# Where the last layer splits its operands: conversions once per step, token operands spread over two steps

## The chip, the cores and the metric

The kernel runs on one core of a Trainium2 chip. The metric is the device time of one execution in microseconds (us), the median of three runs.

## What is computed

Attention with a threshold, a mixture of eight experts, and a gated layer, one after the other. Only the last one, `_moe2_ref`, is touched by the change. Its input is the experts' output, 2304 tokens of width 512.

```python
def reference(**kwargs):
    ...
    attn_out = _attn_ref(**attn_kwargs)
    x = np.ascontiguousarray(attn_out.transpose(0, 2, 1, 3)).reshape(B * S, H * D)
    x = _moe_ref(x=x, **moe_kwargs)
    return _moe2_ref(x=x, **moe2_kwargs)

def _moe2_ref(x, w_gate, w_val, w_out):      # (2304, 512), (512, 1536) twice, (1536, 512)
    g = x @ w_gate
    silu = g * (1.0 / (1.0 + np.exp(-g)))
    val = x @ w_val
    return (silu * val @ w_out).astype(np.float32)
```

## The kernel before, around the change

**Tiling.** `moe2` (line 1533) works on the transposed tokens in groups of 384, taken as three pairs p = 0, 1, 2, and on the 1536 hidden units in 12 slices k of 128. Every float32 operand is split into a high and a low part (names ending in h and l: ScalarE casts the high part, VectorE subtracts to get the low one), so a product of two operands is three matmuls per chunk of 256 rows, and `product` (line 1623) issues six.

**Steps.** The list `steps` is one long sequence. The first 14 steps are `plain` ones (slices 0 to 6 of pair 0, one group each, four products). Then come 29 steps `seven`: slices 7 to 11 of pair 0, then 12 slices each of pairs 1 and 2. A `seven` step does two groups with seven products instead of eight; for that it needs sums of tokens (`ysum`: t1 to t4, from the loaded quarters r0 to r3) and sums of weights (`sums`, on GpSimd, into one buffer sf). The order of its products on TensorE is fixed: tokens y0, y2, yt2, yt1, yt3, y3, yt4 (tiles `p`, only two PSUM banks in turn). Between them stand 18 matmuls of the third product (tiles `o`, function `l2`) for the slice of the step before. A PSUM bank is free for the next product when the VectorE or ScalarE instruction that reads it is done: y0 by the copy at line 1665, y2 by `s<-p,p`, yt2 by `p<-p,p`, yt1 by the copy at line 1680, yt3 by `u<-p,p`, y3 by `s<-p,s`, yt4 by `u<-u,p`.

**Lists.** A `seven` step calls `at(pos)` at the places 0, 1, "u", 2, "t", 3, 4, 5, in this order, and at each of them all that the table `do[i, pos]` holds is issued, so the table sets the order of work on ScalarE, VectorE, GpSimd and the DMA queue (SP). Each engine takes its instructions strictly in that order. The table holds: weights of slice k+3 fetched from DRAM (wf), sums of slice k+2 (sf), the split of slice k+1 (`opers_hi` on ScalarE: ch; `opers_lo` on VectorE: cl; 512 wide for products y0 and y2, 256 wide for yt4, 1024 wide from sf for the other four), and, in the last steps of a pair, loads, sums and splits of the next pair's tokens (`yload`, `ysum`, `yhi`, `ylo`; 768 wide).

**Conversions.** The weights arrive as 64-bit floats. `Weights2.begin` issues, on ScalarE, the high part of a word tile that is ready (oh or ch from wb, line 1476) and the scaling of a raw tile (line 1452); `end` issues, on VectorE, the low part (line 1477) and the three word operations on the tile just scaled (lines 1457 to 1459). In the `seven` steps before the change, places 0 and 3 both do `end`, `begin(1)`, `fill`:

```python
            if i >= n0 and pos in (0, 3):
                w2s.end()
                w2s.begin(1)
                w2s.fill()
```

**Stores.** At slice 11, `store` (line 1592) copies six output tiles out of PSUM and GpSimd issues an indirect DMA for each; two of them use the tag eys, four the tag os.

Of the kernel before, what the change touches and what calls it, by code (L numbers as in the profile page):

```python
# [6 lines left out]
F32 = mybir.dt.float32  # L7
# [607 lines left out]
def apart(tc, group, ins):  # L615

    tc.declare_no_dep(ins.ins, group=group, reason="rows apart")
    tc.add_to_no_dep_group(group, ins.ins)
# [904 lines left out]
GT = 384  # L1523
# [13 lines left out]
def moe2(ctx, tc, w2s, yd, idl, out, y0, py0, pys):  # L1537
    nc = tc.nc
    p = lambda n, b, **kw: ctx.enter_context(tc.tile_pool(name=n, bufs=b, reuse_waits="tile", **kw))
    py, pr, pu, po, pi = p("n_y", 1), p("n_yr", 1), p("n_u", 2), p("n_o", 1), p("n_i", 1)  # L1540
# [5 lines left out]
    idf = pi.tile([128, 18], F32, name="idf")  # L1546
    nc.sync.dma_start(idf[:], idl[0:NTOK, 0:1].rearrange("(t p) o -> p (t o)", p=128))
    idi = pi.tile([128, 18], I32, name="idi")
    nc.vector.tensor_copy(idi[:], idf[:])
    V, S, G = nc.vector, nc.scalar, nc.gpsimd  # L1550
    tt = lambda e, o, a, b, op: e.tensor_tensor(o, a, b, op=op)  # L1551

# [1 line left out]
    Y, R = dict(y0), {}  # L1554

    def yload(p, b):
        R[b, p] = t = pr.tile([128, 2, GT], F32, tag=f"r{b}", name=f"r{b}")
        r, n = 256 * (b // 2), GT * (2 * p + b % 2)
        nc.sync.dma_start(t[:], yd[r:r + 256, n:n + GT].rearrange("(c p) n -> p c n", p=128))

    def ysum(p, n):
        a, b = {"t1": (1, 0), "t2": (3, "t1"), "t3": (3, 1), "t4": ("t2", 2)}[n]

        t = R[1, p] if n == "t3" else R[2, p] if n == "t4" else pr.tile([128, 2, GT], F32, tag="r" + n, name="r" + n)
        tt(V, t[:], R[a, p][:], R[b, p][:], ALU.subtract)
        R[n, p] = t

# [10 lines left out]
    def l2(g, k, order):  # L1578

        uh, ul = H.pop((g, k))  # L1580
        oh, ol = W["o", k]
        if k == 0:
            O[g] = [pso.tile([128, 512], F32, tag="o", name="o") for _ in range(3)]
        for t in range(3):
            sl = slice(128 * t, 128 * t + 128)
            for i, (u, w) in enumerate(((uh, oh), (uh, ol), (ul, oh))):
                nc.tensor.matmul(O[g][t][:], u[:, sl], w, start=k == 0 and i == 0, stop=k == NF - 1 and i == 2)  # L1587
                yield
            if k == NF - 1:
                store(g, t)  # L1590

    def store(g, t):
        i = 3 * g + t
        o = po.tile([128, 512], F32, tag="os", name="os", bufs=4) if i % 3 else pys.tile([128, 512], F32, tag="eys", name="os", bufs=2)
        (S.copy if i % 2 else V.tensor_copy)(o[:], O[g][t][:])
        ins = nc.gpsimd.indirect_dma_start(
            out=out[:, :], out_offset=bass.IndirectOffsetOnAxis(ap=idi[:, i:i + 1], axis=0),
            in_=o[:], in_offset=None, bounds_check=NTOK - 1, oob_is_err=False)
        apart(tc, "out", ins)
# [34 lines left out]
    def plain(g, k, i, at):  # L1634
        res = []
        for nm in (0, 2):
            ps = bank()
            for c in (0, 2):
                product(ps, [t[:, nm + c // 2] for t in w2s.C[k]], Y[c + g % 2, g // 2], c == 0, c == 2)
            res.append(ps)  # L1640
            at(nm // 2)
        s = pu.tile([128, GT], F32, tag=f"s{g % 2}", name="s", bufs=1)
        S.activation(s[:], res[0][:, 0:GT], AF.Silu)
        w2s.begin(2 if i % 2 or i > 11 else 1)
        hidden(g, k, s, res[1][:, 0:GT])()
        w2s.end()
        w2s.fill()
        rest()
        at(2)
        pend.append(l2(g, k, 0))  # L1650
        w2s.done += g
# [60 lines left out]
    steps = []  # L1712
    for k in range(PLAIN + LAG):
        steps += [(g, k - LAG * g) for g in range(2) if 0 <= k - LAG * g < PLAIN]
    n0 = len(steps)
    steps += [(p, k) for p in range(3) for k in range(0 if p else PLAIN, NF)]
    do = defaultdict(list)
    add = lambda i, pos, *what: do[i, pos].append(what)
    for b in (1, 3, 0, 2):
        yload(0, b)  # L1720
    for i, b in ((1, 1), (2, 3)):
        add(i, 2, yhi, 0, b)
        add(i + (b == 1), 0 if b == 1 else 2, ylo, 0, b)
    for i, b in ((n0 - 6, "t1"), (n0 - 5, "t2"), (n0 - 4, "t3")):
        add(i, 0, ysum, 0, b)
        add(i + 1, 0, yhi, 0, b)
        add(i + 1, 2, ylo, 0, b)
    add(n0 - 2, 0, ysum, 0, "t4")
    add(n0, 0, yhi, 0, "t4")
    add(n0, 1, ylo, 0, "t4")  # L1730
# [7 lines left out]
    for i in range(n0, len(steps)):  # L1738
        p, k = steps[i]
        if i + 3 < len(steps):  # L1740
            add(i, 0, w2s.fetch, steps[i + 3][1])
        if i + 2 < len(steps):
            add(i, 2, w2s.sums, steps[i + 2][1])
        if i + 1 < len(steps):
            k1 = steps[i + 1][1]
            for n in (0, 2, 1):
                add(i, 0, w2s.opers_hi, k1, n)
            for n, pos in ((0, 0), (1, 1), (2, "u")):
                add(i, pos, w2s.opers_lo, k1, n)
        if p < 2:  # L1750
            if k == 8:
                for b in (0, 1, 2, 3):
                    add(i, 0, yload, p + 1, b)
            if k > 8:
                add(i, "t", ysum, p + 1, f"t{k - 8}")
            if k == 11:
                for pos, b in ((1, 0), (2, 2), ("t", "t2"), (3, "t1"), (4, "t3")):
                    add(i, pos, yhi, p + 1, b)
                    add(i, pos, ylo, p + 1, b)
                for pos, b in ((0, 3), ("t", "t4")):  # L1760
                    add(i + 1, pos, yhi, p + 1, b)
                    add(i + 1, pos, ylo, p + 1, b)
                add(i + 1, 1, ysum, p + 1, "t4")
    for i, (g, k) in enumerate(steps):
        def at(pos):
            if i >= n0 and pos in (0, 3):
                w2s.end()
                w2s.begin(1)
                w2s.fill()
            for what, *x in do.pop((i, pos), ()):  # L1770
                what(*x)
        (plain if i < n0 else seven)(g, k, i, at)
# [38 lines left out]
def body(tc, q, k, v, tau, emb, mtau, w1, w2, wg, wv, wo, out):  # L1811
    nc = tc.nc
    with ExitStack() as top:
# [100 lines left out]
        with ExitStack() as ctx:  # L1914
            ctx.enter_context(tc.manual_schedule())
            moe2(ctx, tc, w2s, yd, idl, out, y0, py0, c)
# [26 lines left out]
```

## Time and profile before

| | us |
|---|---|
| three runs, median (lowest to highest) | 1081.05 (1079.9 to 1081.9) |
| the profiled execution: its time | 1085.99 |
| its span | 1084.0 |
| TensorE busy in the span | 1028.1 (95%) |
| VectorE, ScalarE, GpSimd busy | 786.0, 576.9, 318.9 |
[...]

The last layer's first plain step begins 604 us into the span. The chain that ended last goes through TensorE for 50% of the span and through VectorE for 9%. A busy TensorE is not TensorE at its peak; what a stage may give is read from its own windows and waits.

### The profile page before, as it was taken

The page shows a single profiled execution, that of the slowest core. Times are in us where ns is not written, and L with a number is a line of the kernel's source. Part 1 is how long each engine was busy: PE and PEld are TensorE (multiplying, and loading weights), DVE is VectorE, ACT ScalarE, POOL GpSimd, SP SyncE. Part 2 cuts the span into 40 slices and gives each one's busy share as a digit, 9 for nine tenths or more (in the row PEclk, how much of TensorE's full clock was granted, in tenths as well). Part 3 has the DMA queues.
Part 4 walks back from the last instruction along what each step waited for, and adds up shares of the span by engine and source line. Part 5 has one row for each costly group of instructions (what it writes and reads, how often), then busy time and mean ns, then how long its engine had stood idle before and what let it go on. Part 6 is the DMA issues. An engine that isn't in the chain of part 4 may idle for free.

```text
span 1084.0 us, 18612 instructions
## 1 busy us (share of the span) xinstructions
PE 1028.1 (95%) x6338; PEld 892.5 (82%) x6338; DVE 786.0 (73%) x1624; ACT 576.9 (53%) x1152; POOL 318.9 (29%) x451
## 2 busy tenths in 40 slices
PE   7999999999998899999999989868899999899996
PEld 6777777776767899999999989757789999799995
DVE  6888888888886445666677458867887778877773
ACT  5777777777772434555565434343454344434432
POOL 6444534446786000000000000211352323442222
PEclk9999999999999999999999989978999999899999
DMA  8679988756832657887897545750122132121101
GB/s 183 157 193 230 204 232 204 191 128 173 229 88 79 206 142 218 223 275 232 235 237 193 159 132 175 243 185 19 40 98 59 40 98 59 49 88 40 40 1 58
DMA packets 141008, 158.12 MB, mean 146 GB/s; under 512 B 53912, under 2 KB 96920, under 8 KB 140912
## 3 DMA queue, kind: packets, MB, share of 16 engines
q1 hardware_dynamic: 138032, 147.47, 50.4%
q0 software_dynamic: 2880, 9.46, 2.3%
q8 instruction: 50, 0.82, 0.3%
q14 instruction: 46, 0.38, 0.1%
HBM read 97.28 MB, written 34.06 MB: 121 GB/s over the span
## 4 chain that ended last, share of the span: by engine, by line
PE 50%; DVE 9%; ACT 3%; issue 2%; DMA 2%; SPq 0%; POOL 0%; POOLq 0%; DVEq 0%; ACTq 0%
PE p L1628 20%; PE o L1587 11%; PE y L1271 9%; PE ph L1253 9%; DVE s L1551 1%; DVE wb L1458 1%; PE pxt L1221 1%; DVE cl L1518 1%; DVE wb L1457 1%; DMA ws<-wb 1%; DVE wb L1459 1%; DMA wf<-ws 0%; ACT uh L1620 0%; DVE u L1551 0%; DVE w1l L1209 0%
## 5 line engine op out<-in xcount | busy, mean ns | idle before, releaser
L1494 POOL TENSOR_TENSOR sf<-wf 128x256 f32<-128x256 f32 x29 | 27.1, 936 | 565.4 <-DVE wb L1459 331.5
L196 DVE TENSOR_REDUCE nmx<-PS 128x1 f32<-128x576 f32 x144 | 108.8, 755 | 53.7 <-PE PS L165 41.3
L230 DVE SCALAR_TENSOR_TENSOR E<-PS,thr,E 128x576 f32<-128x576 f32 x128 | 103.4, 808 | 0.1
L290 ACT COPY h<-PS 128x256 f32<-128x256 f32 (+2 forms) x176 | 67.0, 381 | 66.5 <-PE PS L247 62.7
L220 ACT ACTIVATE E<-PS,nmx 128x576 f32<-128x576 f32 x128 | 96.1, 750 | 4.4 <-DVE nmx L196 2.7
L1258 DVE SCALAR_TENSOR_TENSOR hl<-ph,hh 128x256 fp32r<-128x256 f32 (+5 forms) x64 | 30.9, 483 | 79.8 <-ACT hh L1257 79.8
L165 PE MATMUL PS<-KH,qs 128*128 128x288 f32 x256 | 87.0, 354 | 1.7 <-ACT h L290 1.5
L1587 PE MATMUL o<-ol,uh 128*128 128x512 f32 x216 | 87.3, 404 | 0.0
L1587 PE MATMUL o<-oh,ul 128*128 128x512 f32 x216 | 86.8, 402 | 0.1
L1587 PE MATMUL o<-oh,uh 128*128 128x512 f32 x216 | 86.7, 401 | 0.0
L314 PE MATMUL y<-h,nv 128*64 128x320 f32 (+2 forms) x528 | 86.4, 419 | 0.0
L247 PE MATMUL PS<-ident,E 128*128 128x128 f32 x576 | 85.2, 275 | 1.2 <-DVE E L230 1.0
L1271 PE MATMUL y<-hh,w2h 128*128 128x256 f32 (+5 forms) x256 | 79.4, 310 | 0.0
L165 PEld LDWEIGHTS PS<-KH,qs 128*128 128x128 f32 x256 | 48.5, 190 | 36.9 <-ACT h L290 14.0
L1271 PE MATMUL y<-hl,w2h 128*128 128x256 f32 (+5 forms) x256 | 78.0, 305 | 0.0
L1271 PE MATMUL y<-hh,w2l 128*128 128x256 f32 (+5 forms) x256 | 77.9, 304 | 0.0
L247 PEld LDWEIGHTS PS<-ident,E 128*128 128x128 f32 x576 | 66.6, 140 | 10.4 <-issue 6.9
L165 PE MATMUL PS<-KL,qs 128*128 128x288 f32 x256 | 73.2, 298 | 0.0
L1696 ACT ACTIVATE s<-s 128x384 f32<-128x384 f32 x29 | 15.2, 524 | 106.3 <-DVE s L1551 106.3
L1620 ACT CAST uh<-s 128x384 fp32r<-128x384 f32 x72 | 36.9, 513 | 57.6 <-DVE s L1551 57.2
L1257 ACT ACTIVATE hh<-ph 128x256 fp32r<-128x256 f32 (+5 forms) x64 | 27.7, 433 | 71.1 <-PE ph L1253 67.1
L1551 DVE TENSOR_TENSOR s<-p,s 128x384 f32<-128x384 f32 x72 | 40.3, 559 | 27.2 <-ACT s L1696 16.0
(387 smaller groups left out, 3022.7 us busy)
## 6 DMA issues: line engine op xcount, KB each, us to landing
w1r<-in_moe_w_dram SPq DMA_DIRECT2D x32, 512.0 KB
w2r<-in_moe_w_dram SPq DMA_DIRECT2D x32, 512.0 KB
wf<-ws SPq DMA_DIRECT2D x58, 256.0 KB
xs<-zero SPq DMA_DIRECT2D x8, 1542.0 KB
KH<-tkh SPq DMA_DIRECT2D x60, 144.0 KB
KL<-tkl SPq DMA_DIRECT2D x60, 144.0 KB
rg<-in_moe_w_gate_dram SPq DMA_DIRECT2D x12, 512.0 KB
rv<-in_moe_w_val_dram SPq DMA_DIRECT2D x12, 512.0 KB
```

The lines of the kernel that those rows point to most:

```text
L165: ins = nc.tensor.matmul(S[:, i, a:a + n], x, y, start=first, stop=last)
L196: nc.vector.tensor_reduce(nmx[:], S[:, :, 0:288], axis=AX.XY, op=ALU.max, negate=True)
L220: nc.scalar.activation(e, d["S", s][:, :, 0:288], AF.Exp, bias=d["nm", s][0][:], scale=1.0)
L230: nc.vector.scalar_tensor_tensor(out=e, in0=d.pop(("S", s))[:, :, 0:288], scalar=d.pop(("nm", s))[1][:], in1=e, op0=ALU.is_ge, op1=ALU.mul ...
L247: ins = nc.tensor.transpose(ps[:, o:o + 128], src, self.ident[:])
L290: self.tc.declare_no_dep(self.nc.scalar.copy(o, i).ins, group=f"new1_{g}", reason="the other bank")
L314: nc.tensor.matmul(ps[64 * b:64 * b + 64, p0:p1], v, self.H[i][:, k, o + p0:o + p1], start=c == 0, stop=c == 4 and (p1 == n or c0 == 0))
L1253: nc.tensor.matmul(ps[:, 0:C], w[:, c, o:o + 128], x[:, c, 0:C], start=n == 0, stop=n == 11)
L1271: nc.tensor.matmul(d["y"][c][:, 0:C], w[:, k % 2, sl], h[:, 0:C], start=k == 0 and i == 0, stop=k == 7 and i == 2)
L1551: tt = lambda e, o, a, b, op: e.tensor_tensor(o, a, b, op=op)
L1587: nc.tensor.matmul(O[g][t][:], u[:, sl], w, start=k == 0 and i == 0, stop=k == NF - 1 and i == 2)
L1628: nc.tensor.matmul(ps[:, 0:GT], w[a][:, 128 * c:128 * c + 128], y[b][:, c, :], start=first and m == 0, stop=last and m == 5)
```

## The change

It reorders the lists. (1) In `seven` steps, conversions stand at place 3 alone, as `begin(1)`, `end`, `fill`: one tile per step, not two, and its low part and words in the same place. (2) The token sums t1, t2 move to slice 9 and t3, t4 to slice 10, two per step, one at "t", one at place 4. (3) The splits of the next pair's tokens are spread from place 1 of slice 11 to place 3 of slice 0, each high part some places ahead of its low part. (4) In slice 0, the split of slice 1's weights moves from places 0 to "u" to places 3, 4 and 5. (5) In slices 0 and 11, `sums` stands at place 3, not 2. (6) For pair 0, the splits of r1 and r3 move up by about half a plain step and a whole one; the cast of the token indices moves from the layer's start to a late plain step. (7) t4 gets a tile of its own; the output tag os has 3 buffers, not 4.

```diff
-    nc.vector.tensor_copy(idi[:], idf[:])
...
-        t = R[1, p] if n == "t3" else R[2, p] if n == "t4" else pr.tile([128, 2, GT], F32, tag="r" + n, name="r" + n)
+        t = R[1, p] if n == "t3" else pr.tile([128, 2, GT], F32, tag="r" + n, name="r" + n)
...
-        o = po.tile([128, 512], F32, tag="os", name="os", bufs=4) if i % 3 else pys.tile([128, 512], F32, tag="eys", name="os", bufs=2)
+        o = po.tile([128, 512], F32, tag="os", name="os", bufs=3) if i % 3 else pys.tile([128, 512], F32, tag="eys", name="os", bufs=2)
...
-    for i, b in ((1, 1), (2, 3)):
-        add(i, 2, yhi, 0, b)
-        add(i + (b == 1), 0 if b == 1 else 2, ylo, 0, b)
+    add(n0 - 4, 2, nc.vector.tensor_copy, idi[:], idf[:])
+    for i, pos, fn, b in ((1, 0, yhi, 1), (1, 2, ylo, 1), (1, 2, yhi, 3), (2, 0, ylo, 3)):
+        add(i, pos, fn, 0, b)
...
-            add(i, 2, w2s.sums, steps[i + 2][1])
+            add(i, 2 if 0 < k < 11 else 3, w2s.sums, steps[i + 2][1])
...
-                add(i, 0, w2s.opers_hi, k1, n)
-            for n, pos in ((0, 0), (1, 1), (2, "u")):
+                add(i, 0 if k else 3, w2s.opers_hi, k1, n)
+            for n, pos in ((0, 0), (1, 1), (2, "u")) if k else ((0, 4), (1, 4), (2, 5)):
                 add(i, pos, w2s.opers_lo, k1, n)
...
-            if k > 8:
-                add(i, "t", ysum, p + 1, f"t{k - 8}")
+            if k in (9, 10):
+                for n, pos in enumerate(("t", 4)):
+                    add(i, pos, ysum, p + 1, f"t{2 * k - 17 + n}")
             if k == 11:
-                for pos, b in ((1, 0), (2, 2), ("t", "t2"), (3, "t1"), (4, "t3")):
-                    add(i, pos, yhi, p + 1, b)
-                    add(i, pos, ylo, p + 1, b)
-                for pos, b in ((0, 3), ("t", "t4")):
-                    add(i + 1, pos, yhi, p + 1, b)
-                    add(i + 1, pos, ylo, p + 1, b)
-                add(i + 1, 1, ysum, p + 1, "t4")
+                for j, pos, fn, b in ((0, 1, yhi, 0), (0, "u", yhi, 2), (0, "t", ylo, 0), (0, "t", yhi, "t2"), (0, 3, yhi, "t1"),
+                                      (0, 4, ylo, 2), (0, 4, yhi, "t3"), (0, 5, ylo, "t2"), (0, 5, yhi, 3), (1, 0, ylo, "t1"),
+                                      (1, 0, yhi, "t4"), (1, "u", ylo, "t3"), (1, "t", ylo, 3), (1, 3, ylo, "t4")):
+                    add(i + j, pos, fn, p + 1, b)
...
-            if i >= n0 and pos in (0, 3):
-                w2s.end()
+            if i >= n0 and pos == 3:
                 w2s.begin(1)
+                w2s.end()
                 w2s.fill()
```

Three places show how instructions move. Before, ScalarE's list for slice 8 of pair 0 (ch<-wf and ch<-sf split the weights of the next slice, oh<-wb and ro<-ro are the conversion):

```order
L1665 COPY p_9215<-p 128x384
L1476 CAST oh_9222<-wb 128x512
L1452 ACTIVATE ro<-ro 128x512
L1514 CAST ch<-wf 128x512
L1514 CAST ch<-sf 128x1024
L1514 CAST ch<-wf 128x256
L1670 ACTIVATE s<-s 128x384
L1680 COPY p_9275<-p 128x384
L1476 CAST oh_9304<-wb 128x512
L1452 ACTIVATE ro<-ro 128x512
L1696 ACTIVATE s<-s 128x384
```

Now, the same step:

```order
L1664 COPY p_9212<-p 128x384
L1514 CAST ch<-wf 128x512
L1514 CAST ch<-sf 128x1024
L1514 CAST ch<-wf 128x256
L1669 ACTIVATE s<-s 128x384
L1679 COPY p_9263<-p 128x384
L1476 CAST oh_9287<-wb 128x512
L1452 ACTIVATE ro<-ro 128x512
L1695 ACTIVATE s<-s 128x384
```

The conversion ahead of the weight split is gone; the one behind the second copy stays. Before, VectorE's list in slice 0 of pair 1, from the low part of y3 on:

```order
L1551 TENSOR_TENSOR y3l<-r_9244,y3h 128x768
L1518 TENSOR_TENSOR cl<-wf,ch 128x512
L1551 TENSOR_TENSOR s<-p,p_9723 128x384
L1551 TENSOR_TENSOR r_9242<-rt_9533,r_9242 128x768
L1518 TENSOR_TENSOR cl<-wf,ch 128x256
L1551 TENSOR_TENSOR p_9723<-p,p_9723 128x384
L1518 TENSOR_TENSOR cl<-sf,ch 128x1024
L1595 COPY os<-o 128x512
L1551 TENSOR_TENSOR s<-p_9723,p_9771 128x384
L1551 TENSOR_TENSOR yt4l<-r_9242,yt4h 128x768
```

Now, the end of that step's list:

```order
L1550 TENSOR_TENSOR yt4l<-rt_9552,yt4h 128x768
L1550 TENSOR_TENSOR s<-p,s 128x384
L1518 TENSOR_TENSOR cl<-wf,ch 128x512
L1518 TENSOR_TENSOR cl<-wf,ch 128x256
L1594 COPY os<-o 128x512
L1550 TENSOR_TENSOR s<-p_9765,s 128x384
L1550 TENSOR_TENSOR u_9792<-u_9792,p 128x384
L1550 TENSOR_TENSOR s<-u_9792,s 128x384
L1550 TENSOR_TENSOR ul<-s,uh 128x384 x2
L1518 TENSOR_TENSOR cl<-sf,ch 128x1024
L1594 COPY os<-o 128x512
```

The 1024-wide cl<-sf, which frees sf for the next sums, was the middle of the list and is now all but its last. Before, VectorE's list in plain steps 1 and 2, with the low parts of pair 0's yt4 and y3 (first used by plain step 3):

```order
L1551 TENSOR_TENSOR yt4l<-r_8223,yt4h 128x768
L1551 TENSOR_TENSOR s<-p,s 128x384
L1551 TENSOR_TENSOR ul<-s,uh 128x384
L1477 TENSOR_TENSOR ol_8371<-wb,oh_8370 128x512
L1457 TENSOR_SCALAR wb<-rv 128x512
L1458 SCALAR_TENSOR_TENSOR wb<-rv,wb 128x512
L1459 SCALAR_TENSOR_TENSOR wb<-rv,wb 128x512
L1551 TENSOR_TENSOR y3l<-r_8225,y3h 128x768
```

Now:

```order
L1459 SCALAR_TENSOR_TENSOR wb<-rg,wb 128x512
L1550 TENSOR_TENSOR yt4l<-r_8222,yt4h 128x768
L1550 TENSOR_TENSOR y3l<-r_8224,y3h 128x768
L1550 TENSOR_TENSOR s<-p,s 128x384
L1550 TENSOR_TENSOR ul<-s,uh 128x384
```

The low part of y3 stands six instructions earlier, right behind that of yt4.

## Rows read from the trace of the kernel before

**Rows 1.** Windows: length, PE, PEld, DVE, ACT, POOL busy, granted clock, DMA share, GB/s.

```profile
696.64:767.78 71.14, 53.62 (x232) 47.48 (x231) 53.29 (x86) 25.39 (x47) 17.45 (x20) 0.86 0.36 110
696.64:718.68 22.04, 12.39 (x53) 10.54 (x51) 16.91 (x26) 6.71 (x12) 6.57 (x8) 0.85 0.47 141
767.78:809.93 42.15, 37.34 (x181) 33.08 (x180) 35.69 (x55) 20.77 (x37) 18.89 (x18) 0.96 0.23 76
855.95:867.40 11.45, 11.45 (x61) 10.66 (x60) 8.31 (x15) 4.81 (x9) 3.38 (x4) 1.00 0.15 46
913.21:955.65 42.44, 38.39 (x181) 34.47 (x180) 35.68 (x55) 20.88 (x37) 18.89 (x18) 0.92 0.22 75
```

**Rows 2.** Windows, same columns: plain step 3 with its waits, and an equal step later.

```profile
620.94:631.95 11.01, 7.25 (x25) 6.35 (x24) 4.97 (x8) 2.84 (x5) 0.00 (x0) 0.69 0.64 178
640.31:644.50 4.19, 4.19 (x26) 4.19 (x25) 2.21 (x4) 1.83 (x4) 0.00 (x0) 1.00 0.73 231
```

**Rows 3.** Timeline of TensorE: start, duration (us), instruction, in brackets idle before and releaser.

```profile
709.16 0.69 PE L1628 MATMUL p<-yt1h,ch 128*128 128x384 f32 x1 [6.89 <-DVE s L1551]
...
873.41 0.33 PE L1628 MATMUL p<-yt3h,ch 128*128 128x384 f32 x1
...
925.78 0.69 PE L1628 MATMUL p<-yt4h,ch 128*128 128x384 f32 x1 [3.16 <-DVE u L1551]
```

**Rows 4.** Timeline of VectorE: low part alone, sum beside GpSimd's sums, output copy.

```profile
620.74 0.95 DVE L1551 TENSOR_TENSOR yt4l<-r,yt4h 128x768 fp32r<-128x768 f32 x1
621.61 0.55 DVE L1551 TENSOR_TENSOR s<-p,s 128x384 f32<-128x384 f32 x1
...
896.39 1.50 DVE L1551 TENSOR_TENSOR rt<-r,r 128x768 f32<-128x768 f32 x1
...
1072.33 0.69 DVE L1595 COPY os<-o 128x512 f32<-128x512 f32 x1 [0.62 <-PE o L1587]
```

**Rows 5.** Timeline of ScalarE: plain step 1; slice 7 of pair 0.

```profile
615.95 0.83 ACT L1570 CAST yt4h<-r 128x768 fp32r<-128x768 f32 x1
...
705.50 0.62 ACT L1476 CAST oh<-wb 128x512 fp32r<-128x512 f32 x1 [5.21 <-DVE wb L1459]
```

**Rows 6.** Timeline of VectorE, slice 7 of pair 0.

```profile
704.78 0.69 DVE L1459 SCALAR_TENSOR_TENSOR wb<-ro,wb 128x512 int32<-128x512 int32 x1
707.95 0.69 DVE L1518 TENSOR_TENSOR cl<-wf,ch 128x512 fp32r<-128x512 f32 x1 [2.48 <-ACT ch L1514]
...
715.68 0.68 DVE L1477 TENSOR_TENSOR ol<-wb,oh 128x512 fp32r<-128x512 f32 x1
...
718.07 0.55 DVE L1551 TENSOR_TENSOR s<-p,s 128x384 f32<-128x384 f32 x1
```

**Rows 7.** Timeline of VectorE, a step without extras that starts at 867.40.

```profile
867.51 1.22 DVE L1551 TENSOR_TENSOR ul<-s,uh 128x384 fp32r<-128x384 f32 x2
...
870.92 0.43 DVE L1518 TENSOR_TENSOR cl<-wf,ch 128x256 fp32r<-128x256 f32 x1
...
871.89 1.22 DVE L1518 TENSOR_TENSOR cl<-sf,ch 128x1024 fp32r<-128x1024 f32 x1
```

**Rows 8.** Timeline of GpSimd, slice 11 of pair 1: first and last of the four sums.

```profile
920.71 1.33 POOL L1494 TENSOR_TENSOR sf<-wf 128x256 f32<-128x256 f32 x1 [9.01 <-ACT yt2h L1570]
...
924.41 1.44 POOL L1497 TENSOR_TENSOR sf<-wf,sf 128x256 f32<-128x256 f32 x1
```

**Rows 9.** Timeline of ScalarE, the step that starts at 867.40: weight split, then silu.

```profile
869.53 1.05 ACT L1514 CAST ch<-sf 128x1024 fp32r<-128x1024 f32 x1
...
870.93 0.53 ACT L1670 ACTIVATE s<-s 128x384 f32<-128x384 f32 x1
```

**Rows 10.** Timeline of GpSimd: second and last of the six last stores.

```profile
1073.79 0.97 POOL L1596 DMA_INDIRECT out_dram<-os,idi  x1 [0.30 <-issue]
...
1078.91 0.97 POOL L1596 DMA_INDIRECT out_dram<-os,idi  x1 [0.31 <-issue]
```

More of the change, by code (lines that the diff above doesn't have):

```diff
@@ L1753, in moe2 @@
                     add(i, 0, yload, p + 1, b)
-            if k > 8:
-                add(i, "t", ysum, p + 1, f"t{k - 8}")
+            if k in (9, 10):
+                for n, pos in enumerate(("t", 4)):
+                    add(i, pos, ysum, p + 1, f"t{2 * k - 17 + n}")
             if k == 11:
-                for pos, b in ((1, 0), (2, 2), ("t", "t2"), (3, "t1"), (4, "t3")):
-                    add(i, pos, yhi, p + 1, b)
-                    add(i, pos, ylo, p + 1, b)
-                for pos, b in ((0, 3), ("t", "t4")):
-                    add(i + 1, pos, yhi, p + 1, b)
-                    add(i + 1, pos, ylo, p + 1, b)
-                add(i + 1, 1, ysum, p + 1, "t4")
+                for j, pos, fn, b in ((0, 1, yhi, 0), (0, "u", yhi, 2), (0, "t", ylo, 0), (0, "t", yhi, "t2"), (0, 3, yhi, "t1"),
+                                      (0, 4, ylo, 2), (0, 4, yhi, "t3"), (0, 5, ylo, "t2"), (0, 5, yhi, 3), (1, 0, ylo, "t1"),
+                                      (1, 0, yhi, "t4"), (1, "u", ylo, "t3"), (1, "t", ylo, 3), (1, 3, ylo, "t4")):
+                    add(i + j, pos, fn, p + 1, b)
     for i, (g, k) in enumerate(steps):
         def at(pos):
-            if i >= n0 and pos in (0, 3):
+            if i >= n0 and pos == 3:
+                w2s.begin(1)
                 w2s.end()
-                w2s.begin(1)
                 w2s.fill()
```

## The prediction

> **What bounds the kernel now.** I read the windows by step first, then TensorE's waits in the timeline, then the engine that it waited for. [...] What can be gained lies where steps are longer: slices 7 to 10 of pair 0 take 71.14 us where four steps of 11.45 make 45.8; the two passages from one pair to the next (slices 11, 0 and 1) take 42.15 and 42.44 us where three make 34.35 [rows 1]; and plain step 3 takes 11.01 us where an equal step takes 4.19 [rows 2]. That is 25.3 + 7.8 + 8.1 + 6.8 = 48.0 us in which VectorE or ScalarE, not TensorE, sets the pace. In each of them TensorE's waits end with a VectorE instruction [rows 3]. [...]
>
> All sums below are against the profiled execution (span 1084.0 us, its time 1085.99). The median of the three runs is 1081.05, 4.9 us less; I take the difference that I find off that median.
>
> **Plain step 3 (gain 6.3 us).** It waits for the parts of y3. y3's low part now stands right behind yt4's, so it is ready 0.87 us after it (start to start), at about 620.74 + 0.87 + 0.95 = 622.6 [rows 4]; its high part takes the place on ScalarE where yt4's stood, 615.95 [rows 5]. TensorE needs y3 one product, about a microsecond, after it starts at 620.94. Both waits for y3 go, and with them the low clock. The full difference would be 11.01 - 4.19 = 6.8 [rows 2]; I leave 0.5 for the wait for yt4l, whose place on VectorE has not changed. Low end 3.3, if only the waits go; and all of it can be lost later (rival 1).
>
> **Slices 7 to 10 of pair 0 (gain 13.3 us).** In slice 7 ScalarE stood 5.21 us at a conversion (oh from wb) until VectorE had made the words, and the weight split queued behind it [rows 5]; VectorE then waited 2.48 us for that split [rows 6], and TensorE 6.89 us for the `s<-p,p` behind it [rows 3]. That ring (words, oh, split, cl, bank) is what place 0 made, and it is gone: cl starts when the last word operation is done, 704.78 + 0.7 = 705.5, not 707.95, so TensorE goes on about 2.5 us earlier. Slice 7 then ends near 19.4 instead of 22.04 [rows 1]. The conversion that stays, at place 3, is VectorE's 718.07 - 715.68 = 2.4 us of ol and words [rows 6]; ScalarE's half lies in time in which it is idle. Slice 8: 8.31 + 2.4 = 10.7 us of VectorE fit beside 11.45, plus 0.75 because they stand ahead of the bank's release: 12.2. Slices 9 and 10 each carry two token sums, 0.95 alone and 1.50 beside GpSimd's sums [rows 4]: 8.31 + 2.4 + 0.95 + 1.50 = 13.1 us, VectorE-bound. Sum 19.4 + 12.2 + 13.1 + 13.1 = 57.8 against 71.14. Bounds: 16 (all but slice 7 near 11.45 to 12) and 8 (VectorE waits in each step as well).
>
> **The passages (gain 0.7 and 2.5 us).** The old wait, 3.16 us for a bank behind four low parts and a sum in slice 11 [rows 3], goes: the sums are done in slices 9 and 10, whose VectorE time in pair 1 (8.31 + 0.95 + 1.50 = 10.8) fits; slice 11 keeps two low parts (8.31 + 0.95 + 1.50 = 10.8), fits too. But slice 0 now has five low parts, two output copies and everything else in front of the 1024-wide cl. Work ahead of it: a whole step without that cl, 8.31 - 1.2, plus five times 0.87, plus two copies of 0.69 [rows 4]: about 12.8 us, beginning where the step's two ul end, 1.33 us after its start [rows 7]. It ends some 15.2 us after the step began. What is late next: sf has one buffer, so GpSimd's sums of slice 2 wait for that cl; the four keep GpSimd busy for 3.38 us in a step without extras [rows 1] and last 5.14 in slice 11, beside VectorE's wide work [rows 8]. I take 3.5, since VectorE by then has little left. Then ScalarE's ch from sf and the 256-wide one, 1.40 us [rows 9], then VectorE's 256-wide cl and p, 0.97 [rows 7]: 21.05 us after the start of slice 0. That p frees the bank for product yt3 of slice 1, which TensorE wants at 11.45 + 6.01 (873.41 - 867.40 [rows 3]) = 17.45. So slice 1 is about 3.6 us long, a new wait in place of the old one. It is of the size of the old 3.16, so I charge the clock too: the old passages lost (1 - 0.92) x 42.44 = 3.4 and (1 - 0.96) x 42.15 = 1.7 us to it [rows 1]; I take 2, between 0 and 3.4. Second passage: 34.35 + 3.6 + 2.0 = 39.95 against 42.44, gain 2.5. First: 1.5 more, for VectorE's lag from slice 10 and a last ol; 41.45 against 42.15, gain 0.7. Bounds per passage: +4.5 and -3.
>
> [...]
>
> **The rest.** Moving the cast of the indices, t4's own tile and the place of `sums` I cost at nothing: the cast is off TensorE's path, and GpSimd's start is set by sf's release, not its place; two of the six stores are now ahead of the late sums, four behind them, and the next step's sums wait for sf longer than for those four (1.28 us each, (1078.91 - 1073.79) / 4 [rows 10]). Three os buffers: the last of the six copies at the end must wait until the second store has landed. That one is issued from 1073.79 to 1074.76, the last one from 1078.91 [rows 10]; landing takes up to 4.1 us more (from the last issue's end to the end of the span) and the copy 0.69 [rows 4], so the last store is 0 to 0.7 us late. I take 0.3, a loss.
>
> **Sum.** 6.3 + 13.3 + 0.7 + 2.5 - 0.3 = 22.5 us: 1081.05 - 22.5 = 1058.5.
>
> **The rivals.**
> 1. *The early gain is given back.* Between plain step 3 and slice 7 lie some 65 us in which weights are loaded, converted and written out; if these transfers, not TensorE, set when slice 7 begins, the 6.3 us are only waited out there. For it: VectorE is busy 53.29 of 71.14 us right behind [rows 1], and DMA was busy 0.73 of the later plain step [rows 2]. Against: TensorE has a clock of 1.00 and no gap in that step [rows 2]. Time 1065. Chance 0.15.
> 2. *VectorE still sets slices 7 to 10.* The work is spread, not removed: five conversions in five steps. If its waits on ScalarE stay, half of the 13.3 comes: 1065 too, or 1068 with half of the early gain. Against: 13.1 us is below the 17.8 mean of these steps. Chance 0.14.
> 3. *Slower: the late sums.* [...] Chance 0.05.
> 4. *Nothing.* VectorE's total is unchanged, and if the waits only move, the time stays 1081. Against: 48.0 us of loss with VectorE at 8.31 of 11.45 in the steps around. Chance 0.03.
> 5. *More:* the clock never falls in the passages and slices 8 to 10 fit in 12 us: 6.8 + 16 + 2.7 + 4.5 = 30, 1051. Chance 0.05.
>
> The forecast keeps 0.58. A measurement of this kernel can tell 0.2% (2.2 us) from no change. Faster: 0.58 + 0.15 + 0.14 + 0.05 = 0.92; same 0.03; slower 0.05. The range runs from just under the fifth case to beyond the second with a poor passage: 1050 to 1072.
>
> **What would show it.** In the changed profile: plain step 3 near 4.7 us long with no wait for y3; no ScalarE wait at oh in slices 7 to 11, these four steps near 19, 12, 13, 13; no wait of `yt4` in slice 11; a wait of `yt3` in slice 1 of pairs 1 and 2 of 2 to 4 us, with GpSimd's sums ending only just before it. If that last wait is missing, or if slices 8 to 10 are still 17 us long, the reasons above are wrong.

## The result and the profile after

The changed kernel takes **1062.03 us** (median of four runs, 1061.48 to 1062.81), the kernel before on the same chip 1081.12 (1079.9 to 1081.9): a ratio of 0.9825, 95% interval 0.9808 to 0.9842, so 19.1 us less. The forecast was 1058.5, range 1050 to 1072. The profiled execution took 1061.48 us, with a span of 1059.7 (before: 1085.99 and 1084.0) and a mean granted TensorE clock of 0.993 of full speed (0.979).

The windows by stage, first the plain steps of the kernel before (columns as in [rows 1]):

```profile
603.97:696.64 92.67, 88.91 (x455) 82.52 (x454) 64.46 (x109) 37.74 (x69) 4.09 (x4) 0.96 0.60 180
```

and of the kernel after: plain steps; slices 7 to 10 of pair 0 together, then one by one; first passage; second passage; its slices 0 and 1.

```profile
601.06:686.66 85.60, 85.60 (x456) 80.34 (x454) 64.94 (x110) 37.59 (x69) 4.23 (x4) 1.00 0.65 195
686.66:747.64 60.98, 49.62 (x232) 42.97 (x230) 53.29 (x83) 23.55 (x45) 19.34 (x20) 0.94 0.40 128
686.66:705.55 18.89, 11.61 (x53) 10.02 (x51) 16.18 (x25) 6.13 (x11) 6.99 (x8) 0.91 0.58 190
705.55:719.60 14.05, 13.43 (x60) 11.91 (x60) 11.11 (x18) 5.81 (x12) 3.40 (x4) 0.88 0.69 226
719.60:733.54 13.94, 12.30 (x60) 10.54 (x60) 12.65 (x20) 5.81 (x12) 4.49 (x4) 1.00 0.13 38
733.54:747.64 14.10, 12.27 (x60) 10.50 (x60) 13.36 (x21) 5.80 (x12) 4.47 (x4) 1.00 0.13 39
747.64:789.07 41.43, 37.17 (x181) 31.71 (x182) 35.87 (x57) 22.01 (x40) 16.17 (x17) 1.00 0.25 77
892.34:931.36 39.02, 35.99 (x182) 31.75 (x180) 33.41 (x54) 20.75 (x38) 16.21 (x17) 1.00 0.25 82
903.80:916.63 12.83, 12.22 (x61) 10.55 (x60) 11.96 (x21) 7.06 (x13) 2.02 (x2) 1.00 0.15 47
916.63:931.36 14.73, 12.32 (x62) 10.53 (x60) 11.00 (x19) 5.60 (x11) 10.03 (x11) 1.00 0.39 139
```

Against [rows 1] the plain steps gain 92.67 - 85.60 = 7.1 us, slices 7 to 10 71.14 - 60.98 = 10.2, the passages 0.7 and 3.4: 21.4 in all, the whole difference of the layer (from its first plain step to the end of the span 1084.0 - 603.97 = 480.0 before, 1059.7 - 601.06 = 458.6 after). The rest of the 24.3 us between the two spans lies ahead of the layer, which began 2.9 us earlier. Over the fourteen profiles of this study it begins between 599.8 and 607.5 us, though no kernel differs from another ahead of it; so below, stages and layers are compared, and the medians beside them.

TensorE's waits after: slice 7, slice 10, then slice 0 and twice slice 1 of pair 2.

```profile
696.11 0.69 PE L1627 MATMUL p<-yt1h,ch 128*128 128x384 f32 x1 [4.38 <-DVE s L1550]
...
733.54 0.44 PE L1627 MATMUL p<-y0h,ch 128*128 128x384 f32 x1 [1.16 <-DVE s L1550]
...
912.29 0.45 PE L1627 MATMUL p<-y3l,ch 128*128 128x384 f32 x1 [0.43 <-DVE y3l L1550]
...
921.90 0.45 PE L1627 MATMUL p<-yt1h,ch 128*128 128x384 f32 x1 [0.91 <-DVE s L1550]
...
925.78 0.45 PE L1627 MATMUL p<-yt3h,ch 128*128 128x384 f32 x1 [1.41 <-DVE p L1550]
```

In slice 7 the wait for yt1 is 4.38 us where it was 6.89 [rows 3]. The old wait for yt4 in slice 11 [rows 3] is gone; new are those in slices 0 and 1. Slices 8 to 11 each begin with a wait of 0.63 to 1.92 us for y0, whose bank VectorE frees only behind the conversion. What VectorE does there, in slice 9:

```profile
726.90 1.50 DVE L1550 TENSOR_TENSOR rt<-r,r 128x768 f32<-128x768 f32 x1
...
729.37 1.23 DVE L1477 TENSOR_TENSOR ol<-wb,oh 128x512 fp32r<-128x512 f32 x1
730.53 0.97 DVE L1457 TENSOR_SCALAR wb<-ro 128x512 int32<-128x512 int32 x1
...
732.94 0.55 DVE L1550 TENSOR_TENSOR s<-p,s 128x384 f32<-128x384 f32 x1
```

The conversion takes 732.94 - 729.37 = 3.57 us, not the 2.4 of [rows 6]: ol lasts 1.23 us, not 0.68. And the chain of the late sums, on VectorE, GpSimd (first of four and last), ScalarE and VectorE again:

```profile
918.75 1.22 DVE L1518 TENSOR_TENSOR cl<-sf,ch 128x1024 fp32r<-128x1024 f32 x1
...
920.11 0.73 POOL L1494 TENSOR_TENSOR sf<-wf 128x256 f32<-128x256 f32 x1 [7.02 <-ACT ch L1514]
...
922.62 0.74 POOL L1497 TENSOR_TENSOR sf<-wf,sf 128x256 f32<-128x256 f32 x1
...
923.39 1.05 ACT L1514 CAST ch<-sf 128x1024 fp32r<-128x1024 f32 x1 [3.77 <-POOL sf L1497]
...
924.77 0.48 DVE L1518 TENSOR_TENSOR cl<-wf,ch 128x256 fp32r<-128x256 f32 x1 [2.92 <-ACT ch L1514]
```

Each link stands within about a microsecond of where the prediction put it: cl<-sf ends 919.97 - 903.80 = 16.2 us after slice 0 began (15.2 forecast), the sums take 3.25 us (3.5), and VectorE stands 2.92 us idle for them.

### The profile page after: what moved, and what is told of

It reads as the page before. It is cut to its first block, busy times and chain, and to the rows that moved or that the text cites. A ratio compares the mean times of both kernels' runs of the same rounds, so it can differ in the third digit from the quotient of the medians.

```text
span 1059.7 us, 18615 instructions
## 1 busy us (share of the span) xinstructions
PE 1018.4 (96%) x6338; PEld 881.3 (83%) x6338; DVE 787.6 (74%) x1624; ACT 576.0 (54%) x1152; POOL 320.7 (30%) x451
## 4 chain that ended last, share of the span: by engine, by line
PE 43%; DVE 10%; issue 7%; ACT 3%; DMA 2%; POOL 1%; POOLq 0%; DVEq 0%; SPq 0%; ACTq 0%
PE p L1627 15%; PE ph L1253 9%; PE y L1271 9%; PE o L1586 8%; DVE s L1550 2%; DVE wb L1458 1%; PE pxt L1221 1%; ACT ch L1514 1%; DVE wb L1457 1%; DVE u L1550 1%; DMA w2r<-in_moe_w_dram 1%; DVE ol L1477 1%; DVE p L1550 1%; DMA rv<-in_moe_w_val_dram 1%; DVE wb L1459 1%
## 5 line engine op out<-in xcount | busy, mean ns | idle before, releaser
L1695 ACT ACTIVATE s<-s 128x384 f32<-128x384 f32 x29 | 15.2, 526 | 109.6 <-DVE s L1550 109.6
```

## The experiments

**One part at a time.** e1_early has part (6) of the change alone (the cast of the indices, the early splits of r1 and r3), e2_conv part (1) alone, e3_pass parts (2) to (5) and (7). All three start from the kernel before. e4_conv_both is the kernel before with only the order at both places turned:

```diff
             if i >= n0 and pos in (0, 3):
-                w2s.end()
                 w2s.begin(1)
+                w2s.end()
                 w2s.fill()
```

> The kernel before with part (6) alone: the splits of r1 and r3 moved up, the index cast late. My reading: plain step 3 loses its waits and its low clock and the gain is kept to the end, 7.1 us as in the windows of the change (92.67 to 85.60 us for the plain steps), so about 1074. Rival 1 (the gain is waited out before slice 7): 1081, with the start of slice 7 unmoved against the start of the layer.

> The kernel before with part (1) alone: conversions at place 3 only, begin before end. My reading: the ring words, oh, split is gone and slices 7 to 10 of pair 0 go from 71.1 to about 61 us: about 1071. Rival 2 (VectorE sets these slices by its amount of work, which is unchanged): 1079 to 1081. Rival 4 (waits only move): 1081.

> The kernel before with parts (2) to (5) and (7) alone: token sums two per step, spread splits, late cl from sf. My reading: passages as in the change, 41.4 and 39.0 instead of 42.2 and 42.4 us, so 4 us less: about 1077, perhaps 1 us worse because slice 9 then holds two sums and a conversion. Rival: the passages owe their time to the conversions in pair 0 and to nothing else; then 1081, and the second passage stays at 42.

> The kernel before, conversions still at places 0 and 3, but begin before end, so that the oh on ScalarE never waits for words that VectorE makes in the same place. If that ring was the whole loss: slices 7 to 10 come to 61 to 63 us, total 1071 to 1073. If the number of conversions per step is what matters (each stands ahead of cl or of a bank's release on VectorE): slices 7 and 8 stay above 16 us, total 1076 to 1081.

Measured, against 1084.64 for the kernel before, measured beside them:

| | us | ratio (95%) | layer | slices 7 to 10 | passages |
|---|---|---|---|---|---|
| before (profile) | | | 480.0 | 71.1 | 42.2, 42.4 |
| e1_early | 1077.73 | 0.9939 (0.9922 to 0.9955) | 472.1 | 70.3 | 42.2, 42.2 |
| e2_conv | 1076.83 | 0.9925 (0.9908 to 0.9942) | 472.3 | 61.6 | 44.1, 42.2 |
| e3_pass | 1079.41 | 0.9944 (0.9927 to 0.9961) | 473.0 | 70.5 | 39.0, 39.0 |
| e4_conv_both | 1076.86 | 0.9931 (0.9915 to 0.9948) | 470.4 | 62.4 | 42.2, 42.2 |

The expected times were counted from 1081. Against 1084.64 the four runs are 6.9, 7.8, 5.2 and 7.8 us faster, where about 7, 10, 4 and 8 to 10 were expected.

The windows of e1_early, plain steps and slices 7 to 10:

```profile
602.64:688.43 85.79, 85.79 (x455) 80.31 (x454) 65.49 (x111) 37.73 (x69) 4.07 (x4) 1.00 0.65 195
688.43:758.72 70.29, 53.58 (x232) 47.76 (x231) 52.33 (x84) 25.41 (x47) 17.46 (x20) 0.85 0.35 111
```

The early gain is kept in full: nothing behind it grows, so rival 1 (transfers take it back) is out. The three parts are nearly independent: in the layer they save 8.0, 7.7 and 7.0 us, 22.7 together, and the change 21.4. The missing 1.3 has a place. In the first passage e3_pass takes 39.0 us, e2_conv 44.1, the change 41.4: with one conversion per step, those of slices 10 and 11 move into it. The windows of e2_conv, slices 7 to 10 and first passage, and of e4_conv_both, slices 7 to 10 together, then 7, 8 and 9 one by one; last, e4_conv_both's ScalarE in slice 7:

```profile
695.99:757.54 61.55, 50.08 (x232) 42.86 (x230) 52.96 (x82) 23.56 (x45) 19.07 (x20) 0.94 0.40 131
757.54:801.67 44.13, 37.77 (x181) 33.07 (x181) 37.71 (x58) 22.22 (x40) 18.87 (x18) 0.96 0.22 72
```

```profile
695.19:757.54 62.35, 49.39 (x233) 43.77 (x231) 52.45 (x84) 25.31 (x47) 18.13 (x20) 0.92 0.39 125
695.19:717.03 21.84, 12.04 (x52) 10.52 (x51) 18.36 (x28) 7.36 (x13) 6.59 (x8) 0.84 0.85 278
717.03:732.88 15.85, 13.79 (x60) 11.90 (x60) 13.27 (x22) 6.89 (x14) 3.47 (x4) 0.89 0.14 40
732.88:746.08 13.20, 12.11 (x60) 10.69 (x61) 11.35 (x19) 6.25 (x12) 4.03 (x4) 1.00 0.13 40
```

```profile
703.11 0.62 ACT L1476 CAST oh<-wb 128x512 fp32r<-128x512 f32 x1 [5.22 <-DVE wb L1459]
```

e4_conv_both keeps two conversions per step and still saves 8.8 of the 71.1 us, nearly all of it in slices 8 and 9, which took 19.77 and 17.88 us in the kernel before. What cost time there was the ring words, oh, split, cl, which `end` ahead of `begin` closes within one place. Slice 7 is another matter: it stays at 21.84 us (22.04 before), and ScalarE's wait at oh at 5.22 (5.21 in [rows 5]), because these words are left over from the last plain step and not made in the same place. Here only taking the conversion out of place 0, ahead of the weight split, helps: in e2_conv slice 7 takes 19.56 us. So neither of the two theories on record holds for all four slices. The passages of e4_conv_both stay at 42.2, and its layer gains more than e2_conv's.

**The new wait in slice 1.** Two edits of the changed kernel let the sums start earlier: the first is e5_clsf_place4, the second, with two os buffers instead of three, e6_sf_two_buffers.

```diff
-            for n, pos in ((0, 0), (1, 1), (2, "u")) if k else ((0, 4), (1, 4), (2, 5)):
+            for n, pos in ((0, 0), (1, 1), (2, "u")) if k else ((0, 4), (1, 4), (2, 4)):
...
-    w2s.psum, w2s.pf = p("n_s", 1), p("n_f", 6)
+    w2s.psum, w2s.pf = p("n_s", 2), p("n_f", 5)
```

> The change with one edit: in slice 0 the 1024-wide low part cl<-sf of slice 1 stands at place 4 instead of place 5, so ahead of the five instructions of the hidden group. Theory A (GpSimd's sums, which start only when that cl is done, make slice 1 long): cl ends about 3 us earlier, the sums too, yt3's wait of 1.41 us and yt1's of 0.91 go; slice 1 falls from 14.73 to about 12, while the hidden group 1.2 us later costs slice 0 or slice 1 up to 1 us; each passage 1.5 to 2.5 us shorter, time near 1058 (1057 to 1059). Theory B (VectorE's total in slices 0 and 1 sets them, the sums only fill it): slice 1 stays at 14 or more, the waits move to y0 or y2, and the time is within 1 us of the change, 1062.

> The change with two buffers of the sums tile sf (paid with five instead of six wf buffers and two instead of three os buffers), all orders as in the change. GpSimd then need not wait for slice 1's cl<-sf before it makes the sums of slice 2. Theory A (the sums' start sets slice 1): the sums of slice 2 are done 5 us or more before they are wanted, the ACT wait of 3.77 us at ch<-sf is gone, slice 1 is 11.5 to 12.5 instead of 14.73, each passage 2.2 to 3.2 us shorter; the two os buffers may cost up to 1.5 us at the end: time 1056 to 1059. Theory B (VectorE's total): slice 1 stays above 14, time 1062 to 1064. If the loads with five wf buffers come late, a wait for DMA would stand in slices 1 and 2 of every pair instead, and the run would tell nothing about A.

Measured: 1060.52 us, ratio 0.9817 (0.98 to 0.9833), and 1061.52, ratio 0.9822 (0.9805 to 0.9838); before 1080.45. The second passage of e5_clsf_place4, then of e6_sf_two_buffers, and VectorE's split of yt4 in the slice 0 of the latter:

```profile
892.43:930.67 38.24, 36.03 (x181) 31.81 (x180) 34.51 (x54) 20.86 (x38) 18.39 (x18) 1.00 0.25 84
```

```profile
893.26:931.22 37.96, 36.09 (x182) 31.77 (x180) 34.78 (x54) 20.86 (x38) 18.59 (x18) 1.00 0.26 84
```

```profile
913.79 1.48 DVE L1550 TENSOR_TENSOR yt4l<-rt,yt4h 128x768 fp32r<-128x768 f32 x1
```

The wait for yt3 is gone in both, as theory A has it; but the passage loses only 0.8 and 1.1 us of its 4.7 over three plain lengths of 11.45 (a step without extras, [rows 1]). Slice 1 still takes 13.95 and 13.73 us. Where the sums now run beside it the split of yt4 takes 1.48 us, not 0.95. So A is worth a quarter to a third of slice 1's excess of 3.3 us. In e5_clsf_place4 a part of the gain goes into a new wait for y2, whose bank the hidden group frees, and that group now stands behind cl<-sf:

```profile
918.58 0.45 PE L1627 MATMUL p<-y2h,ch 128*128 128x384 f32 x1 [0.65 <-DVE u L1550]
```

In e6_sf_two_buffers no order was changed, and VectorE is busy 34.78 of 37.96 us; that points to B without proving it. The layers are 457.0 and 458.7 us, against 458.6 for the change: e6_sf_two_buffers takes longer in slice 7 by what its passages gain.

```profile
686.86:708.43 21.57, 13.50 (x52) 11.50 (x51) 19.27 (x26) 6.16 (x11) 12.10 (x12) 0.84 0.54 170
```

With a second buffer three rounds of sums, not two, fall into slice 7, and VectorE beside them is busy 19.27 us, not 16.18; the slice takes 21.57 us, not 18.89.

**Less VectorE work there.** The changed kernel with all copies of pairs 0 and 1 on ScalarE:

```diff
-        (S.copy if i % 2 else V.tensor_copy)(o[:], O[g][t][:])
+        (S.copy if i % 2 or g < 4 else V.tensor_copy)(o[:], O[g][t][:])
```

> The change with the output copies of pairs 0 and 1 all on ScalarE; three of six in each passage stood on VectorE. That takes three times 0.61 us (start to start) off VectorE in slices 0 and 1 and nothing else. VectorE's total sets the passages (theory B): slice 0 and slice 1 together 1.2 to 1.8 us shorter, each passage near 37.5 instead of 39.0 and 40 instead of 41.4, time near 1059. The late sums alone set slice 1 (theory A): the sums start earlier only by the two copies ahead of cl<-sf, 1.2 us, and slice 1 gains at most that, slice 0 nothing. ScalarE, busy 7.06 and 5.60 us in the two slices, has room for the copies; should its new place in the queue delay ch or the silu, the passages stay at 39.

Measured: 1063.27 us against 1084.34, ratio 0.9796 (0.9774 to 0.9817). Slices 0 and 1 of pair 2:

```profile
909.10:921.20 12.10, 11.90 (x61) 10.49 (x60) 11.16 (x19) 8.24 (x16) 2.65 (x2) 1.00 0.13 45
921.20:935.62 14.42, 12.10 (x62) 10.46 (x60) 10.52 (x17) 5.79 (x12) 10.04 (x11) 1.00 0.48 145
```

Slice 0 gains 0.73 us, which the late sums alone could not give it, and slice 1 0.31; the waits of 0.9 and 1.4 us in slice 1 stay, since cl<-sf ends only 0.3 us earlier against the start of that slice. The two gains make 1.04 us, a little less than theory B's 1.2 to 1.8. So each theory holds a part. Both edits together, in the last two runs below, bring the second passage to 36.96: 2.06 less, where one by one they gave 0.78 and 1.04. What the other 2.6 us above three plain lengths are made of was not tested.

**The place of the conversion.** In the changed kernel `pos == 3` becomes `pos == "t"` (e7_conv_place_t) or `pos == 4` (e8_conv_place_4).

> The change with the conversion at place t (behind the product of yt1, ahead of VectorE's u<-p,p) instead of place 3. There VectorE idles 1.08 us in slice 8, waiting for TensorE. Theory C (slices 8 to 10 are a ring of VectorE and TensorE in which the conversion stands ahead of the release of the y3 bank, and the idle microsecond counts): slices 8 to 10 take 13.0 to 13.3 instead of 14.05, 13.94, 14.10, so 2 to 3 us in all, time 1059 to 1060. Theory D (VectorE's own work of 12.65 to 13.36 us sets slices 9 and 10, wherever the conversion stands): those two gain at most 1.0 together, time 1061 to 1062.

> The change with the conversion at place 4, that is behind s<-p,s, which frees the bank for y0, and ahead of the hidden group, which frees the bank for y2. Theory C (the ring): y0's waits of 0.63 to 1.17 us go, but u<-u,p comes about 3 us after its product and y2's wait grows from 0.3 to 0.5 to about 1.5: slices 8 to 10 between 13.3 and 14.1, time 1060 to 1062.5. Theory D (VectorE's own work): the waits move from y0 to y2 one for one, 1062. If the conversion's place matters little in both runs, what sets these slices is the sum of the work and not its order.

Measured: 1062.7 us, ratio 0.9834 (0.9812 to 0.9855), and 1061.77, ratio 0.9829 (0.9813 to 0.9845). Slices 8 to 10 take 14.27, 15.69, 14.25 at "t" and 14.61, 13.36, 14.21 at place 4, against 14.05, 13.94, 14.10. TensorE's wait in slice 9 at "t", then at the start of slice 10 at place 4:

```profile
733.12 0.45 PE L1627 MATMUL p<-yt4h,ch 128*128 128x384 f32 x1 [2.46 <-DVE u L1550]
```

```profile
733.97 0.44 PE L1627 MATMUL p<-y2h,ch 128*128 128x384 f32 x1 [2.02 <-DVE u L1550]
```

At "t" the conversion holds up `u<-p,p` and so the bank for yt4; at place 4 it holds up `u<-u,p` and the bank for y2. Theory C's gain of 2 to 3 us is refuted: VectorE is only moved from one release to another. Slices 9 and 10 together take 1.9 us more at "t" and 0.5 less at place 4; the layers take 459.7 and 459.4 us, against 458.6.

**The sums beside VectorE.** The changed kernel with GpSimd's four sums left out in slices 8 to 10 of pair 0, a fill with zeros in their place:

```diff
-            add(i, 2 if 0 < k < 11 else 3, w2s.sums, steps[i + 2][1])
+            add(i, 2 if 0 < k < 11 else 3, w2s.nosums if p == 0 and 8 <= k <= 10 else w2s.sums, steps[i + 2][1])
...
+    def nosums(self, k):
+        s = self.S[k] = self.psum.tile([128, 4, 256], F32, tag="sf", name="sf")
+        self.nc.gpsimd.memset(s[:], 0.0)
```

> The change with GpSimd's four sums replaced by one fill with zeros in slices 8, 9 and 10 of pair 0, and only there (slices 10 and 11 of pair 0 and slice 0 of pair 1 then work with zeros for sf). What VectorE does is the same. Contention (the sums beside it make VectorE's wide splits and conversions longer): ol 0.7 us instead of 1.22, the conversion 2.4 instead of 3.0 to 3.6, VectorE's busy time in slices 9 and 10 about 1.2 us less, and these two steps 13.0 to 13.3 instead of 13.94 and 14.10; time about 1060. Order alone (the ring sets these slices, and the sums cost nothing): the steps stay within 0.3 us of 13.9 and 14.1, time 1062.

Measured: 1061.68 us, ratio 0.978 (0.9758 to 0.9802). The interval lies clear of that of the change (0.9808 to 0.9842). Slices 9 and 10, then slice 9: GpSimd's fill, and VectorE's token sum beside it, conversion and release of y0's bank:

```profile
722.65:735.19 12.54, 12.09 (x61) 10.54 (x61) 11.16 (x20) 5.81 (x12) 0.96 (x1) 1.00 0.13 42
735.19:747.92 12.73, 12.09 (x61) 10.54 (x61) 11.81 (x21) 5.82 (x12) 0.96 (x1) 1.00 0.15 43
```

```profile
729.61 0.96 POOL L1501 MEMSET sf<- 128x1024 f32 x1 [11.65 <-DVE cl L1522]
...
729.88 0.95 DVE L1554 TENSOR_TENSOR rt<-r,r 128x768 f32<-128x768 f32 x1
...
732.06 0.69 DVE L1477 TENSOR_TENSOR ol<-wb,oh 128x512 fp32r<-128x512 f32 x1
732.66 0.42 DVE L1457 TENSOR_SCALAR wb<-ro 128x512 int32<-128x512 int32 x1
...
734.52 0.55 DVE L1554 TENSOR_TENSOR s<-p,s 128x384 f32<-128x384 f32 x1
```

This settles it for slices 9 and 10. With the sums away the same conversion takes 734.52 - 732.06 = 2.46 us, ol 0.69 and the first word operation 0.42, and the two steps are 1.4 us shorter each. Slice 8, at the same clock of 0.88, gains only 0.3 (13.79 us). Beside the sums three of VectorE's instructions in slice 9 are each about 0.55 us longer (0.95 to 1.50, 0.69 to 1.23, 0.42 to 0.97). The two of them with two inputs are 0.55 and 0.54 us longer, the word shift, which has one, 0.55; beside the fill, which reads nothing, the token sum takes 0.95. By what mechanism the sums lengthen them no run shows.

**Conversions out of these steps.** The changed kernel with the edits of e5 and e10, and more conversions begun in the plain steps (e11_conv_earlier; in e12_conv_earliest the new expression is `2 if i else 1`):

```diff
-        w2s.begin(2 if i % 2 or i > 11 else 1)
+        w2s.begin(2 if i % 3 or i > 11 else 1)
```

> The change with e5's and e10's edits, and two conversions begun in two of three plain steps instead of every other one, so that of the words of five conversions in the seven-product steps two come ahead of slice 7 and only slices 7 and 8 carry one, slice 9 an ol. Theory D (VectorE's own work sets slices 8 to 10): slice 9 near 12, slice 10 near 11.6 (8.3 + 0.95 + 1.5 = 10.8 us of VectorE), slice 11 and slice 0 of the first passage as in the second; slices 7 to 10 near 56 instead of 61, both passages near 37; time 1051 to 1054. Against it: if DMA, busy 0.65 of the plain steps, or VectorE there (64.94 of 85.60 us) becomes the limit, the plain steps or slice 7 take the gain back: 1057 or more.

> As the run before it, with two conversions begun in every plain step from the second on: slice 7 alone has the words of one, slice 8 an ol. Theory D: slices 9 and 10 near 11.5 to 11.8, slice 8 near 12, slices 7 to 10 near 53; time 1049 to 1053 if the plain steps stay at 85.6. If loads set the pace of the plain steps, waits for DMA stand in them or in slice 7, and this run is slower than the one before it.

Measured, against 1084.34: 1061.67 us, ratio 0.9791 (0.9768 to 0.9815), and 1062.56, ratio 0.9793 (0.9775 to 0.9811). The windows of e11_conv_earlier, plain steps, slices 7 to 10 and second passage, then its waits: TensorE, ScalarE twice, VectorE.

```profile
604.10:696.16 92.06, 87.91 (x455) 81.76 (x454) 69.03 (x117) 39.04 (x72) 4.42 (x4) 0.98 0.65 198
696.16:753.63 57.47, 48.92 (x232) 43.09 (x231) 50.11 (x79) 23.73 (x45) 19.17 (x20) 0.94 0.34 110
...
894.18:931.14 36.96, 35.82 (x182) 31.76 (x180) 32.70 (x51) 22.32 (x41) 18.47 (x18) 1.00 0.26 86
```

```profile
690.30 0.44 PE L1627 MATMUL p<-yt4h,ch 128*128 128x384 f32 x1 [3.02 <-DVE s L1550]
...
680.75 0.67 ACT L1452 ACTIVATE rg<-rg 128x512 f32<-128x512 f32 x1 [4.25 <-DMA rg<-in_moe_w_gate_dram]
...
688.80 0.67 ACT L1452 ACTIVATE ro<-ro 128x512 f32<-128x512 f32 x1 [3.21 <-DMA ro<-in_moe_w_out_dram]
...
685.64 0.43 DVE L1457 TENSOR_SCALAR wb<-rg 128x512 int32<-128x512 int32 x1 [1.43 <-DMA ws<-wb]
```

Where the conversions left, the steps fell as theory D has it: slice 10 to 11.8 us, the first passage to 37.27. But 1051 to 1054 us was missed in the way that the expectation allowed for: the plain steps went from 85.60 to 92.06. ScalarE waits at the head of its list for raw weights that have not landed (from 662 us to the end of these steps its waits for them sum to 11.0 us; in the change they sum to 4.2 in all of the plain steps); VectorE once waits 1.43 us for a word tile that is still being written out; and TensorE waits 3.02 us for VectorE. In e12_conv_earliest the plain steps take 93.41 us and slice 7 takes 22.49. The layer is 455.4 us with two in three and 458.6 with two in each, against 458.6 for the change. e11_conv_earlier has the lowest layer of the kernels that leave nothing out; by the ratios it is not to be told from the change, as the intervals overlap. The edits of e5 and e10 without the third were not run.

## Why the prediction was right, and which terms were off

- **Plain step 3**, 6.3 forecast, 7.1 found in the plain steps. The waits for y3 went as foreseen (one of them, 0.60 us for the high part, had ended with ScalarE, not with VectorE). The 0.5 left for yt4l's wait was not needed: with the cast of the indices, which had waited 5.09 us for its load, gone from the head of VectorE's list, yt4l starts 15.8 us after the layer did and not 16.8. So its move was probably worth something, where the prediction costs it at nothing; no run moved it alone.
- **Slices 7 to 10**, 13.3 forecast, 10.2 found: the largest error. Slice 7 came out as worked (19.4 forecast, 18.9 found); slices 8 to 10 took 14.05, 13.94 and 14.10 us where 12.2, 13.1 and 13.1 were forecast. The mis-sized term is "The conversion that stays, at place 3, is VectorE's 718.07 - 715.68 = 2.4 us": the row was of an instruction without GpSimd beside it. One of the token sums was priced beside the sums, the conversion was not; beside them it is 3.0 to 3.6. Without them slices 9 and 10 take 12.54 and 12.73 us in e9, close to 13.1 less the 0.55 charged for that token sum. In slice 8 the sums explain only 0.3 of the 1.9 us that were missed. Another 0.6 is the clock: 14.05 us at 0.88 in this profile, 13.49 and 13.48 at a clock of 1.00 in e5 and e10, whose orders there are the same. The other 1 us is open.
- **Passages**, 0.7 and 2.5 forecast, 0.7 and 3.4 found. The rows of the late sums came as written, to about a microsecond (the terms given for the end of cl<-sf, 1.33 + 12.8 + 1.2, make 15.3, not 15.2). Two terms were wrong and by luck nearly cancelled: the 2 us for the clock, the author's estimate from the two old passages (behind the new waits of 0.91 and 1.41 us the clock stayed at 1.00), and no excess for slice 0 (it took 1.4 over 11.45 in the second passage, 2.5 in the first). One sign did not come: the wait for yt3 in slice 1 is 1.41 us, not 2 to 4, since slice 0 was itself longer and 0.91 us were already waited for yt1. The mechanism named for slice 1, the sums, is only a part of the truth: an earlier start of the sums gave the second passage 0.8 and 1.1 us (e5, e6), and fewer copies on VectorE gave it 1.0 with the sums almost as late as before (e10).
- **The tail**, 0.3 forecast, none found: the last copy waited 2.26 us for its buffer, but the last store was issued 1.28 us after its predecessor, as before.
- **Rivals.** 1 is refuted by e1_early. 2 (VectorE still sets slices 7 to 10) was true in part, at 3 of its 6.6 us, by VectorE's own work and not by the waits on ScalarE that it named. 3 did not come: the passages took 41.43 and 39.02 us, at a clock of 1.00. 4 and 5 fell with the measured time.
- **The median**: the 21.4 us of the layer against 22.5 forecast is within 5%; the medians differ by 19.1. The profiled execution of before was 4.9 us above its median, and its layer began 2.9 us later than that of after; how the layer of a median execution compares no profile shows, so the difference is left open.

## What to carry to other kernels

Price an instruction from a row in which the same neighbours run: a conversion beside GpSimd's sums cost up to half again what it cost alone (3.57 us against 2.46). Where one instruction's wait holds up those behind it on its engine, as ScalarE's 5.21 us at oh did here [rows 5], look for a ring closed within one place of the list (here words, oh, split, cl); turning two calls broke it in slices 8 and 9 and gave most of what halving the conversions per step gave (8.8 us of 9.6). And where an edit removes a wait of 1.4 us and gains 0.8, look for the wait that came in its place (0.65 us for y2 in e5): here the wait that ended last was one of several limits, and the edits that gave 0.8 and 1.0 us per passage alone gave 2.1 together.

## What the runs showed of the hardware

- Waits of 0.91 and 1.41 us in one step left the granted clock at 1.00 (slice 1; three passages of 39.0 us, in the change and in e3_pass), where the old one of 3.16 went with 0.92 over three steps [rows 1, 3].
- The sums lengthened also a VectorE operation with one input, the word shift, from 0.42 to 0.97 us. A fill on GpSimd beside it left a token sum at 0.95 us, where the sums made it 1.50.
- The same instructions in slice 8 ran once at a clock of 0.88 and twice at 1.00 (14.05 against 13.49 us); what decides it behind slice 7's wait of 4.4 us stays open. The low stretch had not gone in e5 and e10: their slice 11 ran at 0.88 and took 13.88 and 13.89 us, against 12.78 at 1.00 in the change, with the same waits of 1.2 us ahead of it and 0.5 in it. Slices 8 and 11 of e5:

```profile
706.66:720.15 13.49, 12.33 (x61) 10.55 (x61) 11.05 (x18) 5.82 (x12) 3.38 (x4) 1.00 0.68 235
...
748.17:762.05 13.88, 13.41 (x60) 12.15 (x61) 12.32 (x19) 9.29 (x16) 4.47 (x4) 0.88 0.12 38
```
